# A four-layer attention network on one core: masks loaded as ready bfloat16 with the key weights asked for first, and two weight prefetches of the last block issued from SyncE

## The chip, the core and the metric

The kernel runs as one program on 1 core of one Trainium2 chip. The metric is the device time of one execution in microseconds, the median over runs. TensorE (PE) multiplies, VectorE (DVE) and ScalarE (ACT) do elementwise work, GpSimd (POOL) does elementwise work and issues DMAs through its own queue, and SyncE (SP) does nothing but issue DMAs. Each engine executes its instructions in order, so an instruction that waits holds up all that stand behind it on that engine.

## The reference

The input is a 2048 x 512 float32 sequence. Four layers follow each other, A, B, A, B, each added to its input after a layer norm:

```python
x = x + _A_ref(_layernorm(x), A_wq, A_wk, A_wv, A_wo)
x = x + _B_ref(_layernorm(x), B_wq, B_wk, B_wv, B_wo, B_beta)
x = x + _A_ref(_layernorm(x), A_wq, A_wk, A_wv, A_wo)
x = x + _B_ref(_layernorm(x), B_wq, B_wk, B_wv, B_wo, B_beta)
```

Layer A is full attention with 32 heads of 16 columns that share one key and one value head: `softmax(q k^T / 4) v`, all 2048 queries against all 2048 keys. Layer B cuts the sequence into 4 blocks of 512, does causal attention inside a block for each of 32 heads, and adds a linear attention over the blocks before it: a memory `M` of `phi(k)^T v` with its normaliser `z`, mixed in by a gate `sigmoid(beta)` for each head.

## The kernel before, in words

The sequence is worked in 4 blocks of 512 rows. Products that need float32 accuracy are made of three matmuls over rounded parts (high times high, high times low, low times high; `project`, L481), so each weight exists as a pair in a tile `w`: the rounded copy made by POOL (L204) and the rest, which DVE subtracts (L306, and L339 and L340 for the keys and values of layer A). `wload` loads a weight once through a staging tile `wst` (a pool of two buffers), splits it, and stores the pair in DRAM (`wd`, L310). Later uses load the pair back with one 512 KB DMA from POOL's queue (L293) into one of six `w` buffers. `wprefetch(n)` issues loads until n weights are ready, and `wget` hands them out in the order of one list.

The Python program emits instructions with a small clock model of its own (`clk`, `pe`, `on`), by which generators are interleaved (`par`, `weave`); a scheduler then sets each engine's order. Four stretches of time follow.

- The head. SP loads the first block of x, then constants (L217 to L239): an identity and selectors as `cs`, and masks and norm patterns as float32 in `wst` staging tiles, which DVE casts to bfloat16 tiles (L224 to L240). The key and value weights of layer A come after them in eight small-run DMAs (L336). Then `prep` runs: the layer norm of block 0 (`norm_stats` L516 to L530, `norm_tiles`: subtract and scale L538, transpose on PE L541, high part L544, low part L549), loads of x for the next block with its statistics, then `a_keys` (projection, split L577 and L579, the key tile `kst` L605 and L606, the values L611 and a bound on the norms L618) and `a_queries` of block 0 (four weights Aq0 to Aq3; split; the parts go to DRAM as `sd`, L656, with a guard row `mr`, L632 and L635). `a_load` fetches the head pairs of queries from `sd` as `qa` (L699, L700), and with them the first scores start (L101, L104), then the exponentials (ACT, L790).
- The body. For each block of queries ACT evaluates 128 exponentials of 128x1024 while PE multiplies; layer B of the block before is woven in beside.
- The last block of layer B (`side(NB - 1, 1, None, True)`), which has no layer A left beside it: `out_norm`, then `b_block` with `last=True`. There `begin()` projects q and k of the first head tile (`inputs(0)`), sends their parts to DRAM as `sb` (L931), loads the first head pair back as `qkb` (`b_load`, L971) and takes row maxima (L1001); `beside()` projects the values of the last two tiles and does `inputs(1)`. `par` picks among generators that are ready the one that keeps PE's tiling; one that is named `urgent` goes first. After both, `wprefetch(2)` asks for the weights Bq2 and Bk2.
- The eight head pairs of that block, the output projection (`out_norm` of `otb`), and the store.

The program uses eight completion semaphores in turn for the DMAs of SP, so each of them also waits for the landing of the eighth before it.

Of the kernel before, what the change touches and what calls it, by code (L numbers as in the profile page):

```python
# [29 lines left out]
F32 = mybir.dt.float32  # L30
# [24 lines left out]
C_ID, C_BM, C_SEL, C_MQ, C_MK, C_BN, C_BK, C_MV = 0, 128, 136, 144, 656, 784, 912, 1040  # L55
# [5 lines left out]
def shape_constants():  # L61
# [26 lines left out]
    return c  # L88
# [3 lines left out]
def net_kernel(ctx, tc, x_in, a_wq, a_wk, a_wv, a_wo, b_wq, b_wk, b_wv, b_wo, b_beta, cst, out):  # L92
# [76 lines left out]
    def st(shape, dt, tag):  # L169
        return one.tile(shape, dt, tag=tag, name=nm(tag))  # L170

    def tmp(n, shape, dt, tag):
        return pools[n].tile(shape, dt, tag=tag, name=nm(tag))

    def f(ap):
        return ap.bitcast(F32)
# [39 lines left out]
    cs = st([P, C_MQ], F32, "cs")  # L216
    nc.sync.dma_start(cs, cst[:, 0:C_MQ])  # L217
    c1 = tmp(2, [P, 512], F32, "wst")
    nc.sync.dma_start(c1, cst[:, C_MQ:C_MK])
    c2 = tmp(2, [P, 512], F32, "wst")[:, 0:C_MV - C_MK]  # L220
    nc.sync.dma_start(c2, cst[:, C_MK:C_MV])
    ident = cs[:, C_ID:C_ID + P]
    maskq = st([P, 512], BF16, "maskq")
    V.tensor_copy(maskq, c1)  # L224
    bmask = cs[:, C_BM:C_BM + 8]
    sel = [cs[:, C_SEL + i:C_SEL + i + 1] for i in range(7)]
    idb = st([P, P], BF16, "idb")
    V.tensor_copy(idb, ident)
    maskk = st([P, P], BF16, "maskk")
    V.tensor_copy(maskk, c2[:, C_MK - C_MK:C_MK - C_MK + P])  # L230
    bnq = st([P, 4, 32], BF16, "bnq")
    V.tensor_copy(bnq.rearrange("p t h -> p (t h)"), c2[:, C_BN - C_MK:C_BN - C_MK + P])
    bnk = st([P, P], BF16, "bnk")
    V.tensor_copy(bnk, c2[:, C_BK - C_MK:C_BK - C_MK + P])
    maskv = st([P, 4, P], BF16, "maskv")
    maskw = st([P, 4, P], BF16, "maskw")
    for m_, at in ((maskv, C_MV), (maskw, C_MW)):
        c3 = tmp(2, [P, 512], F32, "wst")
        nc.sync.dma_start(c3, cst[:, at:at + 512])  # L239
        V.tensor_copy(m_.rearrange("p c k -> p (c k)"), c3)  # L240
# [42 lines left out]
    def wload(kind, i, w=None, parts=""):  # L283
# [6 lines left out]
        if (kind, i) in parts_d:  # L290
            if w is None:
                w = tmp(6, [P, 2, 512], F32R, "w")
            G.dma_start(f(w), parts_d[kind, i])  # L293
            wq_["ready"].append((kind, i, w))
            return
# [21 lines left out]
    ahead_ = [2]  # L317

# [14 lines left out]
    w0 = tmp(2, [P, 512], F32, "wst")  # L333
    for r in range(8):
        src = (a_wv if r == 7 else a_wk).rearrange("(k p) c -> p k c", p=P)
        nc.sync.dma_start(w0.rearrange("p (k r c) -> p k r c", k=4, r=8)[:, :, r, :], src,  # L336
                          allow_slow_non_contiguous=True)
# [3 lines left out]
    nc.sync.dma_start(wkv_d, f(w1))  # L341
# [807 lines left out]
    def b_block(b, last, exact, norms):  # L1149
# [52 lines left out]
        yield from par(begin(), beside())  # L1202
        ahead_[0] = 2
        if last:
            wprefetch(2)
        if last:
            layout("b")
# [13 lines left out]
    def everything(exact):  # L1221
# [21 lines left out]
        def prep():  # L1243
            for b in range(NB):
                if exact:
                    xt, st_ = load_x(b), None
                elif b == 0:
                    xt, st_ = x_0, None
                else:
                    xt, st_ = ahead.pop(b)  # L1250
                for tiles in ((0, 1), (2, 3)) if st_ is None else ((0, 1, 2, 3),):
                    yield from norm_tiles(xt, tiles, clk["pe"] + LOAD, st_)
                if b < NB - 1 and not exact:
                    xt = load_x(b + 1)
                    ahead[b + 1] = xt, norm_stats(xt, (0, 1, 2, 3), clk["pe"] + LOAD)
                yield from a_keys(L, b, aw)
                if b == 0 or exact:
                    yield from a_queries(L, b, aw, not exact)
                evac_on[0] = "dve"
# [117 lines left out]
```

## Time and profile before

| | |
|---|---|
| median of 3 runs | 3129.34 us (3118.13 to 3132.39) |
| the profiled execution | 3124.81 us, span 3123.0 us |
| first matmul of the key projection (L481) | starts at 21.03 us |
| first scores of layer A (L101) | start at 46.28 us |
| first exponential (ACT L790) | starts at 47.22 us |
| last row of layer A's exponentials | starts at 2926.52 us |
| PE without work in the last block | 7.55 us, until 2979.24 us |
| mean granted PE clock | 0.976 |

Times in the timeline are from the span's start. A row gives start, duration, engine, line, operation and tiles, the number of instructions merged into it, and in brackets how long the engine was idle before it and what released it. Durations of pipelined instructions overlap: the step from one start to the next is the real cost of one in a run of equal ones.

### The profile page before, as it was taken

How to read it: one execution, taken by the hardware profiler on the slowest of the kernel's cores; microseconds unless marked ns; L12 is line 12 of the kernel's file. 1: busy time of each engine (PE TensorE's matmuls, PEld its weight loads, DVE VectorE, ACT ScalarE, POOL GpSimd, SP SyncE). 2: the span in 40 equal slices, each digit the busy share in tenths (PEclk: the TensorE clock that was granted, in tenths of full speed). 3: DMA queues.
4: the chain of work that ended last, by engine and by line, in shares of the span. 5: the costliest groups of instructions: out<-in, count | busy, mean ns of one | idle time of the engine just before them, and what ended most of it. 6: DMA issues, size and time to landing. Idle time of an engine off the chain costs nothing.

```text
span 3123.0 us, 115586 instructions
## 1 busy us (share of the span) xinstructions
PE 2776.1 (89%) x51746; PEld 1324.5 (42%) x51746; DVE 1581.4 (51%) x4515; ACT 2323.0 (74%) x2519; POOL 278.4 (9%) x437
## 2 busy tenths in 40 slices
PE   6899888999898998889998898988998899898977
PEld 3444443445443453344544344434443445343543
DVE  6644345534555435564455545456345643555465
ACT  4788777886788767787688878668688887888433
POOL 2001120001000010000100010000000001000111
PEclk9999999999999999999999999999999999999978
DMA  5212231113311233112422142311331113211331
GB/s 156 79 53 81 91 121 47 40 61 108 102 40 42 68 106 95 39 43 71 136 78 73 38 137 96 122 48 51 115 97 45 42 30 127 66 42 46 127 106 38
DMA packets 153596, 242.30 MB, mean 78 GB/s; under 512 B 26272, under 2 KB 101888, under 8 KB 153088
## 3 DMA queue, kind: packets, MB, share of 16 engines
q1 hardware_dynamic: 124672, 132.03, 14.2%
q0 software_dynamic: 28416, 102.77, 10.3%
q8 instruction: 407, 6.67, 0.9%
q14 instruction: 101, 0.83, 0.1%
HBM read 164.21 MB, written 70.52 MB: 75 GB/s over the span
## 4 chain that ended last, share of the span: by engine, by line
PE 38%; ACT 24%; issue 18%; DVE 10%; DMA 6%; POOL 2%; SPq 1%; DVEq 0%; ACTq 0%; POOLq 0%
ACT pa L790 20%; PE bank L101 18%; PE bank L481 13%; PE bank L104 7%; ACT pa L1066 3%; DVE mo L1030 3%; DMA sb<-parts 3%; DMA xt<-in_A_x_dram 1%; DVE parts L579 1%; DMA qkb<-sb 1%; POOL parts L577 1%; DMA wst<-in_B_wk_dram 0%; PE bank L541 0%; DVE qf L559 0%; DVE m L1001 0%
## 5 line engine op out<-in xcount | busy, mean ns | idle before, releaser
L790 ACT ACTIVATE pa<-bank 128x1024 f32<-128x1024 f32 x2048 | 1952.1, 1041 | 458.2 <-PE bank L104 451.9
L104 PE MATMUL bank<-pa,va 64*17 64x512 f32 x14336 | 1101.9, 598 | 0.0
L101 PE MATMUL bank<-pa,va 64*17 64x512 f32 x2048 | 1057.7, 597 | 8.6 <-DVE ts L828 8.0
L101 PE MATMUL bank<-qa,kst 49*32 49x512 f16 x2048 | 741.5, 381 | 159.2 <-ACT pa L790 108.2
L104 PE MATMUL bank<-qa,kst 49*32 49x512 f16 x14336 | 816.8, 386 | 1.9 <-DVE qmx L634 1.9
L1030 DVE CUSTOM_DVE_ANT_0 mo<-bank,maskq 128x256 bf16<-128x256 f32 (+3 forms) x896 | 438.6, 490 | 297.6 <-PE bank L104 239.8
L104 PEld LDWEIGHTS <-kst 49*32 49x32 f16 x14336 | 224.3, 90 | 502.5 <-issue 490.9
L101 PE MATMUL bank<-qkb 48*32 48x384 f16 (+6 forms) x1472 | 331.3, 305 | 94.7 <-DVE m L1030 33.7
L1066 ACT ACTIVATE pa<-bank 128x1024 f32<-128x1024 f32 x320 | 317.4, 1033 | 82.9 <-PE bank L104 79.7
L104 PE MATMUL bank<-qkb 48*32 48x512 f16 (+7 forms) x6720 | 354.1, 311 | 12.4 <-DVE m L1001 10.8
L101 PEld LDWEIGHTS <-kst 49*32 49x32 f16 x2048 | 172.3, 91 | 382.6 <-issue 354.3
L481 PE MATMUL bank<-xh,w 128*128 128x512 f32 x832 | 296.9, 416 | 9.7 <-DVE w L339 4.5
L104 PEld LDWEIGHTS bank<-pa,va 64*17 64x17 f32 x14336 | 256.7, 94 | 26.1 <-DVE t L829 12.1
L481 PE MATMUL bank<-w,xh 128*128 128x512 f32 x752 | 244.6, 407 | 3.7 <-issue 2.0
L101 PEld LDWEIGHTS bank<-pa,va 64*17 64x17 f32 x2048 | 187.7, 94 | 105.4 <-issue 16.7
L104 PEld LDWEIGHTS <-qkb 50*32 50x32 f16 (+1 forms) x6720 | 151.1, 93 | 186.2 <-issue 177.7
L293 POOL DMA_DIRECT2D w<-wd x154 | 85.4, 554 | 1390.8 <-PE bank L481 1207.9
L481 PEld LDWEIGHTS bank<-xh,w 128*128 128x128 f32 x832 | 158.9, 191 | 85.3 <-issue 41.8
L101 PEld LDWEIGHTS <-qkb 48*32 48x32 f16 (+1 forms) x1472 | 123.5, 93 | 130.2 <-issue 86.3
L559 DVE COPY qf<-bank 128x512 f32<-128x512 f32 x91 | 62.8, 690 | 213.9 <-PE bank L481 213.9
L104 PE MATMUL bank<-pa,vb 128*17 128x384 f32 (+3 forms) x1920 | 165.3, 447 | 4.0 <-ACT pa L1066 3.6
L481 PE MATMUL bank<-xl,w 128*128 128x512 f32 x416 | 167.6, 403 | 0.2 <-DVE xl L549 0.2
(171 smaller groups left out, 2679.3 us busy)
## 6 DMA issues: line engine op xcount, KB each, us to landing
w<-wd POOLq DMA_DIRECT2D x154, 512.0 KB, 5.0
sb<-parts SPq DMA_DIRECT2D x192, 128.0 KB
qkb<-sb SPq DMA_DIRECT2D x256, 96.0 KB
wd<-w POOLq DMA_DIRECT2D x24, 512.0 KB, 4.0
x<-xt SPq DMA_DIRECT2D x48, 256.0 KB
xt<-x SPq DMA_DIRECT2D x48, 256.0 KB
qa<-sd SPq DMA_DIRECT2D x176, 66.0 KB
xt<-in_A_x_dram SPq DMA_DIRECT2D x40, 256.0 KB
```

Source lines behind the costliest of these rows:

```text
L101: nc.tensor.matmul(*a, **k)
L104: tc.keep_in_program_order(nc.tensor.matmul(*a, **k))
L293: G.dma_start(f(w), parts_d[kind, i])
L481: T.matmul(ps, lhsT=l_(kt), rhs=r_(kt), start=n == 0, stop=n == 11)
L559: V.tensor_copy(x, ps)
L577: G.tensor_scalar(parts[:, 0, :], x, up, 0.0, op0=ALU.mult, op1=ALU.add)
L579: V.scalar_tensor_tensor(parts[:, 1, :], x, up, parts[:, 0, :], op0=ALU.mult, op1=ALU.subtract)
L790: A.activation(x, sc, AF.Exp, scale=scale)
L1030: V.tensor_tensor_reduce(out=mo[:, 0:nk], in0=ps[:, o_:o_ + nk], in1=maskq[:, 512 - nk:512], op0=ALU.add, op1=ALU.max, scale=1.0, scalar=- ...
L1066: A.activation(e, sc, AF.Exp, scale=0.25 if exact else 0.25 / (UPB * UPB))
```

## The change

Four things change in the code.

1. The constants. The host packs all masks and the bfloat16 identity as bfloat16 pairs into float32 words (`shape_constants`), so that `cst` has 576 bytes of float32 and 4096 bytes of bfloat16 for each of 128 partitions, where it had 8256 bytes of float32. Two loads bring them straight into two tiles, `halves`: a small one with the identity, `maskk`, `bnq` and `bnk`, and a large one with `maskq`, `maskv` and `maskw`. The seven casts on DVE are gone, and the names are now views of these tiles.
2. The key and value weights of layer A. They come right after the small constants, ahead of the large masks, in five DMAs instead of eight: for each of the four row tiles one DMA writes the 16 key columns seven times (a source with a step of 0), and one DMA brings the values. The staging tile `w0` is now the first user of its pool. The store of the split pair (`wkv_d`) moves from right behind the split into `prep`, behind the load of block 1.
3. `prep`. The statistics of the next block (`norm_stats`) are emitted after `a_keys` and `a_queries` of this block; the loads of its x stay where they were.
4. The last block. `begin()` is passed to `par` as `urgent`, and the prefetch of two weights after it (Bq2 and Bk2) is issued from SP instead of POOL.

```diff
+C_ID, C_BM, C_SEL, C_HALF = 0, 128, 136, 144
+C_IB, C_MK, C_BN, C_BK, C_MQ, C_MV = 144, 272, 400, 528, 656, 1168
...
-    cs = st([P, C_MQ], F32, "cs")
-    nc.sync.dma_start(cs, cst[:, 0:C_MQ])
-    c1 = tmp(2, [P, 512], F32, "wst")
-    nc.sync.dma_start(c1, cst[:, C_MQ:C_MK])
...
-    V.tensor_copy(maskq, c1)
...
-    for m_, at in ((maskv, C_MV), (maskw, C_MW)):
-        c3 = tmp(2, [P, 512], F32, "wst")
-        nc.sync.dma_start(c3, cst[:, at:at + 512])
-        V.tensor_copy(m_.rearrange("p c k -> p (c k)"), c3)
...
+    nc.sync.dma_start(halves[0][0], cst[:, halves[0][1]:halves[1][1]])
+    w0 = tmp(2, [P, 512], F32, "wst")
+    w0_ = w0.rearrange("p (k r c) -> p k r c", k=4, r=8)
+    for k in range(4):
+        src = bass.AP(tensor=a_wk.tensor, offset=a_wk.offset + k * P * DH, ap=[[DH, P], [0, 7], [1, DH]])
+        nc.sync.dma_start(w0_[:, k, 0:7, :], src, allow_slow_non_contiguous=True)
+    nc.sync.dma_start(w0_[:, :, 7, :], a_wv.rearrange("(k p) c -> p k c", p=P), allow_slow_non_contiguous=True)
+    nc.sync.dma_start(halves[1][0], cst[:, halves[1][1]:halves[1][1] + (C_N - C_MQ) // 2])
+    small, masks = (x.bitcast(BF16) for x, _ in halves)
...
-            G.dma_start(f(w), parts_d[kind, i])
+            (nc.sync if w_sync[0] else G).dma_start(f(w), parts_d[kind, i])
...
-        yield from par(begin(), beside())
+        first = begin()
+        yield from par(first, beside(), urgent=first if last else None)
         ahead_[0] = 2
         if last:
+            w_sync[0] = True
             wprefetch(2)
+            w_sync[0] = False
...
                     xt = load_x(b + 1)
-                    ahead[b + 1] = xt, norm_stats(xt, (0, 1, 2, 3), clk["pe"] + LOAD)
+                    t_ = clk["pe"] + LOAD
+                    if b == 0:
+                        nc.sync.dma_start(wkv_d, w1.bitcast(F32))
                 yield from a_keys(L, b, aw)
                 if b == 0 or exact:
                     yield from a_queries(L, b, aw, not exact)
+                if b < NB - 1 and not exact:
+                    ahead[b + 1] = xt, norm_stats(xt, (0, 1, 2, 3), t_)
```

The order of instructions shows what moves. In the head, SP's queue before, from the constants on (`wst_161` is the key and value weight, `gv` the gate, `xt_319` to `xt_325` block 1 of x):

```order
L217 DMA cs_89<-in_cst_dram 128x144
L219 DMA wst_91<-in_cst_dram 128x512
L221 DMA wst_93<-in_cst_dram 128x384
L349 DMA gv_174<-in_B_beta_dram 128x1x1 x4
L239 DMA wst_107<-in_cst_dram 128x512
L239 DMA wst_110<-in_cst_dram 128x512
L349 DMA gv_174<-in_B_beta_dram 128x1x1 x3
L336 DMA wst_161<-in_A_wk_dram 128x4x16 x7
L336 DMA wst_161<-in_A_wv_dram 128x4x16
L349 DMA gv_174<-in_B_beta_dram 128x1x1
L211 DMA xt_319<-in_A_x_dram 128x512
```

and the same stretch now, where `wst_94` is the key and value weight and lines have shifted by a few:

```order
L221 DMA cs_89<-in_cst_dram 128x144
L226 DMA halves_6_91<-in_cst_dram 128x256
L231 DMA wst_94<-in_A_wk_dram 128x7x16 x4
L232 DMA wst_94<-in_A_wv_dram 128x4x16
L233 DMA halves_7_92<-in_cst_dram 128x768
L346 DMA gv_152<-in_B_beta_dram 128x1x1 x8
L215 DMA xt_297<-in_A_x_dram 128x512
```

The weight now stands ahead of the large masks and the gates, and nothing that it waits for on DVE stands before it. On DVE in the head, the subtraction that finishes Aq0 (`w_205`) and Aq1 (`w_212`) before:

```order
L516 BN_STATS s_115_334<-xt_323 128x6
L359 RECIPROCAL over_186<-over_186 128x8
L306 TENSOR_TENSOR w_205<-wst_203,w_205 128x512
L517 BN_AGGR mv_327<-s_115_334 128x2
L516 BN_STATS s_116_337<-xt_325 128x6
L517 BN_AGGR mv_327<-s_116_337 128x2
L519 TENSOR_SCALAR ve_340<-mv_327 128x4
L521 TENSOR_SCALAR sh_342<-ve_340 128x4
L523 TENSOR_SCALAR yi_344<-sh_342 128x4
L306 TENSOR_TENSOR w_212<-wst_210,w_212 128x512
```

and now (`w_183` is Aq0, `w_190` Aq1, `xt_303` the last tile of block 1, `kmx_180` the bound on the keys):

```order
L513 BN_STATS s_156_676<-xt_303 128x6
L608 COPY va_15_111<-bank 128x4x16
L514 BN_AGGR mv_666<-s_156_676 128x2
L516 TENSOR_SCALAR ve_679<-mv_666 128x4
L615 TENSOR_REDUCE kmx_180<-bank 128x1
L308 TENSOR_TENSOR w_183<-wst_181,w_183 128x512
L308 TENSOR_TENSOR w_190<-wst_188,w_190 128x512
L576 SCALAR_TENSOR_TENSOR parts_323<-qf_318,parts_323 128x512
```

Both subtractions now stand together, behind all four statistics of block 1 and behind the two readings of the key projection; Aq0's stood in front of the fourth before. In the last block, POOL's queue before, from the second tile's key weight on (`w_52294` is Bk1, `w_52686` and `w_52688` are Bq2 and Bk2, `w_53021` and `w_53084` Bq3 and Bk3):

```order
L293 DMA w_52294<-wd_5945 128x1024
L293 DMA w_52686<-wd_6239 128x1024
L577 TENSOR_SCALAR parts_52283<-qf_52281 128x512
L293 DMA w_52688<-wd_6622 128x1024
L577 TENSOR_SCALAR parts_52310<-qf_52308 128x512
L293 DMA w_53021<-wd_7564 128x1024
L293 DMA w_53084<-wd_8046 128x1024
```

and SP's queue now at the same place (`w_52665` and `w_52667` are Bq2 and Bk2, `sb_52265` the parts of q and `sb_52292` those of k of the first head tile):

```order
L858 DMA xt_55077<-x_173 128x512
L295 DMA w_52665<-wd_6218 128x1024
L928 DMA sb_52265<-parts_52262 8x16x512 x3
L295 DMA w_52667<-wd_6601 128x1024
L928 DMA sb_52292<-parts_52289 8x16x512 x3
L968 DMA qkb_19_119<-sb_52265 48x2x512 x2
```

The two loads have left POOL and stand on SP in front of the stores that the first row maxima wait for. On PE the rows of the last block are the same as before, word for word up to the numbers of the names, so `urgent` moves nothing there.

More of the change, by code (lines that the diff above doesn't have):

```diff
@@ L53 @@
 TA1 = 110e3
-C_ID, C_BM, C_SEL, C_MQ, C_MK, C_BN, C_BK, C_MV = 0, 128, 136, 144, 656, 784, 912, 1040
+C_ID, C_BM, C_SEL, C_HALF = 0, 128, 136, 144
+C_IB, C_MK, C_BN, C_BK, C_MQ, C_MV = 144, 272, 400, 528, 656, 1168
 S_X, S_H, S_L, S_G = 0, 4, 5, 6
@@ L87, in shape_constants @@
         c[64 * i + 48, C_SEL + S_G] = -GUARD_K
-    return c
+    c[:, C_IB:C_IB + P] = np.eye(P)
+    u = np.ascontiguousarray(c[:, C_HALF:]).view(np.uint32)
+    u = ((u + 0x7fff + ((u >> 16) & 1)) >> 16).astype(np.uint16)
+    return np.concatenate([c[:, 0:C_HALF], u.view(np.float32)], axis=1)
 @with_exitstack
@@ L215, in net_kernel @@
     x_0 = load_x(0)
-    cs = st([P, C_MQ], F32, "cs")
-    nc.sync.dma_start(cs, cst[:, 0:C_MQ])
-    c1 = tmp(2, [P, 512], F32, "wst")
-    nc.sync.dma_start(c1, cst[:, C_MQ:C_MK])
-    c2 = tmp(2, [P, 512], F32, "wst")[:, 0:C_MV - C_MK]
-    nc.sync.dma_start(c2, cst[:, C_MK:C_MV])
+    cs = st([P, C_HALF], F32, "cs")
+    nc.sync.dma_start(cs, cst[:, 0:C_HALF])
+    halves = []
+    for a, z in ((C_IB, C_MQ), (C_MQ, C_N)):
+        h_ = st([P, (z - a) // 2], F32, f"halves{a}")
+        halves.append((h_, C_HALF + (a - C_HALF) // 2))
@@ L222, in net_kernel @@
+    small, masks = (x.bitcast(BF16) for x, _ in halves)
     ident = cs[:, C_ID:C_ID + P]
-    maskq = st([P, 512], BF16, "maskq")
-    V.tensor_copy(maskq, c1)
     bmask = cs[:, C_BM:C_BM + 8]
     sel = [cs[:, C_SEL + i:C_SEL + i + 1] for i in range(7)]
[L227 to L236, printed above, removed]
-    for m_, at in ((maskv, C_MV), (maskw, C_MW)):
-        c3 = tmp(2, [P, 512], F32, "wst")
-        nc.sync.dma_start(c3, cst[:, at:at + 512])
-        V.tensor_copy(m_.rearrange("p c k -> p (c k)"), c3)
+    idb, maskk = small[:, 0:P], small[:, P:2 * P]
+    bnq, bnk = small[:, 2 * P:3 * P].rearrange("p (t h) -> p t h", t=4), small[:, 3 * P:4 * P]
@@ L241, in net_kernel @@
+    maskq = masks[:, 0:512]
+    maskv = masks[:, 512:1024].rearrange("p (c k) -> p c k", c=4)
+    maskw = masks[:, 1024:1536].rearrange("p (c k) -> p c k", c=4)
     ones = st([P, 32], BF16, "ones")
@@ L317, in net_kernel @@
     ahead_ = [2]
+    w_sync = [False]
     def wget(kind, n, ahead=None):
@@ L332, in net_kernel @@
     wkv_d = dram.tile([P, 2, 512], F32, tag="wkv_d", name="wkv_d")
[L333 to L337, printed above, removed]
     w1 = tmp(6, [P, 2, 512], F32R, "w")
@@ L340, in net_kernel @@
     V.tensor_tensor(w1[:, 1, :], w0, f(w1[:, 0, :]), op=ALU.subtract)
-    nc.sync.dma_start(wkv_d, f(w1))
     wq_["ready"].append(("Akv", 0, w1))
```

## The prediction

> **What bounds the kernel now.** I read the page first (span, busy shares), then the stretches in time, then the timeline and the chain of waits at the two ends.
>
> ```profile
> span 3123.0 us, 115586 instructions
> PE 2776.1 (89%) x51746; PEld 1324.5 (42%) x51746; DVE 1581.4 (51%) x4515; ACT 2323.0 (74%) x2519; POOL 278.4 (9%) x437
> L790 ACT ACTIVATE pa<-bank 128x1024 f32<-128x1024 f32 x2048 | 1952.1, 1041 | 458.2 <-PE bank L104 451.9
> ```
>
> PE is busy for 89% of the span, and the 2048 exponentials wait almost only for PE. This body is left as it was: past the first 100 us and up to the last block the order of all engines is the old one. What can change is when the body starts, and how long the last block takes after it. At the start, the stretches and the timeline:
>
> ```profile
> 10.00:20.00 10.00, 3.94 (x16) 3.06 (x16) 7.57 (x30) 2.35 (x4) 1.55 (x2) 1.00 0.58 105
> ```
>
> ```profile
> 14.07 3.71 SPq L336 DMA_DIRECT2D wst<-in_A_wk_dram  x7
> 15.21 2.67 DVE L549 TENSOR_TENSOR xl<-bank,xh 128x512 fp32r<-128x512 f32 x4
> 16.57 0.59 ACT L544 CAST xh<-bank 128x512 fp32r<-128x512 f32 x1 [0.27 <-PE bank L541]
> 20.45 0.43 DVE L339 CAST w<-wst 128x512 fp32r<-128x512 f32 x1 [2.58 <-DMA wst<-in_A_wv_dram]
> 21.03 0.77 PE L481 MATMUL bank<-xh,w 128*128 128x512 f32 x1 [4.50 <-DVE w L339]
> 46.28 0.61 PE L101 MATMUL bank<-qa,kst 49*32 49x512 f16 x1 [2.29 <-DMA qa<-sd]
> ```
>
> (Columns of the stretches: length, then busy time of PE, its weight load, DVE, ACT and POOL, granted PE clock, DMA share, GB/s.) Between 10 and 20 us PE works for 3.94. The normalised block is complete when ACT ends at 16.57 + 0.59 = 17.16, but the first projection waits until 21.03 for a weight whose first load was issued at 14.07. The scores start at 46.28. At the other end:
>
> ```profile
> 2961.02 0.53 POOL L293 DMA_DIRECT2D w<-wd  x1 [14.96 <-PE bank L481]
> 2962.36 4.82 SPq L931 DMA_DIRECT2D sb<-parts  x6
> 2963.59 0.58 POOL L293 DMA_DIRECT2D w<-wd  x1 [1.25 <-PE bank L481]
> 2965.68 1.23 POOL L293 DMA_DIRECT2D w<-wd  x2 [0.85 <-PE bank L481]
> 2966.17 10.23 DMA sb<-parts
> 2979.24 0.58 PE L101 MATMUL bank<-qkb 48*32 48x512 f16 x1 [7.55 <-DMA qkb<-sb]
> ```
>
> The fifth row is of the chain of waits: the last store of the first head tile's parts, issued at 2966.17, takes 10.23 us to land, the load behind it comes later still, and PE has nothing to do for 7.55 us.
>
> **Part by part, the head.** The change removes seven casts and moves the weight loads forward. (The third row is of the chain of waits.)
>
> ```profile
> 0.74 1.82 SPq L211 DMA_DIRECT2D xt<-in_A_x_dram  x4
> 11.66 1.00 DVE L538 TENSOR_SCALAR xn<-xt,mv,yn 128x512 f32<-128x512 f32 x2
> 17.83 2.51 DMA wst<-in_A_wv_dram
> 20.92 0.69 DVE L340 TENSOR_TENSOR w<-wst,w 128x512 fp32r<-128x512 f32 x1
> 26.24 0.59 ACT L557 COPY qf<-bank 128x512 f32<-128x512 f32 x1 [2.81 <-PE bank L481]
> ```
>
> SP has issued x at 2.56; two constants, then five weight DMAs at the old 3.71 / 7 = 0.53 each, or half as much again for their wider shape, end at 6.1 to 7.5, and with the 2.51 us that the last of them took to land the weight is there at about 10. DVE asks for it only behind the first two scalings, 11.66 + 1.00, so 2.7 us of slack cover a slower load. On DVE seven casts go, three of them as wide as the one of 0.43 at 20.45, and that one and the 0.69 behind it come in before the last scaling; I call that even. So the first projection can start at about 17.2, when ACT's last high part is there, and not at 21.03: 3.8 us earlier. It took from 21.03 to 26.24, 5.2 us; its result then reaches ACT at 22.4.
>
> The next link is the four query weights.
>
> ```profile
> 26.27 0.64 DVE L306 TENSOR_TENSOR w<-wst,w 128x512 fp32r<-128x512 f32 x1
> 28.90 0.69 DVE L516 BATCH_NORM_STATS2 s<-xt 128x6 f32<-128x512 f32 x1 [1.90 <-DMA xt<-in_A_x_dram]
> 30.61 1.15 DVE L306 TENSOR_TENSOR w<-wst,w 128x512 fp32r<-128x512 f32 x1
> 31.19 0.63 ACT L651 ACTIVATE sqq<-qf 128x512 bf16<-128x512 f32 x1
> 31.96 0.68 DVE L618 TENSOR_REDUCE kmx<-bank 128x1 f32<-128x512 f32 x1
> 33.30 0.84 DVE L605 TENSOR_SCALAR xn<-parts,cs 128x512 f32<-128x512 f16 x1
> 34.18 0.75 DVE L606 SCALAR_TENSOR_TENSOR kst<-parts,cs,xn 128x512 f16<-128x512 f16 x1
> 35.94 0.67 DVE L632 TENSOR_SCALAR mr<-bank 8x512 f16<-8x512 f32 x1
> 36.61 0.67 DVE L579 SCALAR_TENSOR_TENSOR parts<-qf,parts 128x512 f16<-128x512 f32 x1
> 37.31 3.52 DMA sd<-parts
> ```
>
> ```profile
> 12.96 0.17 DVE yn L530
> 3039.86 4.91 PE bank L481 x21
> ```
>
> Before, the second subtraction (30.61) stood behind statistics that waited for x until 28.90. Now both stand behind the key bound: ACT copies the keys to 23.0 and squares them (0.63), PE multiplies (0.4, an estimate), DVE reduces (0.68): 24.8; two subtractions of 0.64 end at 26.1, where the second ended at 31.76. From there DVE's own queue is the path: parts 0.67, 0.84 and 0.75 for the key tile, ten dependent small steps like the one at 12.96, 0.2 with the way to the next (2.0), then guard row, its maximum and one scaling (0.67, 0.67, 0.54), then the query parts (0.67): 32.9. PE needs the two query projections meanwhile, 12 matmuls at 4.91 / 21 = 0.234, 2.8 us each, and is done in time. The store behind those parts was issued at 37.31; now it can be at 33.0. Landing, the load back and the first scores follow as before, so they start 4.3 us earlier, near 42. **Head: -4.3 us.** As PE and ACT are then fed in the old way, I take it as kept to the end.
>
> What is moved past what: SP's load of x for the later queries now stands in front of the second store of parts and of the first `qa` loads, and waits for a scaling on DVE that comes right before those parts; it adds its issue alone, about 0.4 us. The gates come later and their exponential stands in ACT's queue before the key copy; by the issue times above the loads end by about 14 (an estimate), and ACT asks at 17.2. The bounds: at best the key path gives the 5.6 us by which the second weight is earlier; at worst x of block 1 is late (the fourth rival, +1.6). Views in place of tiles, the packed constants and the later `wkv_d` store cost nothing: the casts' readers read the same bfloat16, and the store's reader comes hundreds of microseconds later.
>
> **Part by part, the last block.** `urgent` changes no row on PE, so it is priced at nothing. The two loads of 512 KB leave POOL for SP.
>
> ```profile
> DMA packets 1950, 4.09 MB, mean 273 GB/s; under 512 B 177, under 2 KB 1214, under 8 KB 1949
> q0 software_dynamic: 822, 3.01, 62.5%
> q1 hardware_dynamic: 1127, 1.06, 24.9%
> ```
>
> These are the queues from 2962 to 2977: POOL's moved 3.01 MB, SP's 1.06, of which the six stores of 128 KB are 0.79. Before, the stores shared the engines with POOL's loads all along, at 1.06 MB in 15 us = 71 GB/s. Now SP's queue holds load, three stores, load, three stores (1.83 MB), and POOL's next load comes only behind its issue at 2965.68, 1.23 us long, so that its data start about 2967. Up to there SP's queue is alone: 4.5 us from 2962.4 at 273 GB/s are 1.2 MB, that is the first load, three stores, and some of the second load. The 0.6 MB left are 0.2 of load and 0.39 of stores. The stores in company take 0.39 / 71 = 5.5 us, the rest 0.7: landed at about 2973.2, where it was 2976.4. **Last block: -3 us.** Bounds: nothing gained, since the bytes are the same, or -5 if the engines share more evenly; +3.8 if both loads merely stand in front of the stores, 2 x 0.52 MB at 273 GB/s. The loads also wait on SP for a free buffer, until 2961.02 and 2963.59, with the stores queued behind; those parts leave POOL and DVE only at 2962.3 and later, so the waits cost at most the 0.4 us of an issue.
>
> The shorter stall could also spare PE its slow clock.
>
> ```profile
> 44.00:46.00 2.00, 0.00 (x0) 0.00 (x0) 0.27 (x1) 0.59 (x1) 0.59 (x1) 1.00 0.61 190
> 46.00:48.00 2.00, 1.72 (x19) 0.73 (x20) 0.84 (x2) 0.78 (x1) 0.87 (x2) 0.55 0.94 315
> 2974.00:2976.00 2.00, 0.00 (x0) 0.00 (x0) 0.00 (x0) 0.00 (x0) 0.00 (x0) 0.71 1.00 306
> 2980.00:3000.00 20.00, 16.69 (x437) 8.20 (x423) 17.79 (x39) 3.95 (x5) 0.00 (x0) 0.50 0.24 70
> ```
>
> In the head, 2.3 us without matmuls were enough for a clock of 0.55 behind them, so the 4.5 us that I leave in the last block keep it halved, as from 2974 on: no gain. The Trainium skill, "TensorE: Matmul & The Clock Gate", Part 1, says that the clock halves after an idle window of about 3.4 us that runs free; by that a stall of 4.5 us would hold a whole window one time in three, and the sum would be the larger one of the third rival. The row at 46.00 speaks against it.
>
> **The sum.** -4.3 - 3.0 = -7.3 us. The profiled execution took 3124.81 for a span of 3123.0; the 1.8 us around it stay. So 3117.5 on that scale; the median of the runs lies 4.5 above it, and 3129.3 - 7.3 gives **3122.0**. A measurement of this kernel can tell about 0.5%, 15.6 us, from no change.
>
> **The rivals.**
>
> 1. The queue does not matter (chance 0.20). For it: the same bytes go through the same 16 engines, which were 1.00 busy at 2974. Against: POOL's queue was empty before 2965.68. The stall stays 7.55, the head gives its 4.3: 3125. It is what the Trainium skill says in "DMA: Bandwidth & Descriptors", section "Issuing engines are not separate DMA queues": several issuing engines interleave on the same DMA engines, and only issue time is saved. The fifteen microseconds at 273 GB/s agree that they interleave; how a queue's own order tells, no row here shows.
> 2. The loads stand in the way (0.08). On SP they go out ahead of the stores, which wait their 3.8 us: 3129. For it: the stores are in the same queue. Against: the first load has over a microsecond's start.
> 3. The stall shrinks below what lowers the clock (0.14). From 2980 to 3000, at clock 0.50, DVE was busy 17.79, so at most 2.2 us were PE's alone, and about 1 more behind 3000. With the best ends, -5.6 - 5 - 3.2 = -13.8: 3115.5.
> 4. Slower (0.08): the statistics of block 1 now stand in front of both subtractions. If the last tile of x lands where it did, at 28.9 and not near 20 (issued by 17, and 2.5 to 3.5 us on the way as in the rows above), DVE reaches the subtractions at 31 and ends the second at 32.3; the 6.8 us of queue behind it bring the store to 39 and the scores to 47.9, +1.6, and with a last block unchanged 3131. It decides from a landing at about 23 on; then DVE waits for x instead of the key projection. For it: SP holds eight small gate loads in front of x, each waiting for the eighth DMA before it. Against: by my times those loads are over by about 14, and the x buffers are free before 17.2.
>
> **How the numbers follow.** The forecast has 0.50. The range holds rivals 1, 2, 4 and the forecast with the scatter of the three runs shown, and part of rival 3: 3110 to 3132. Faster by over 0.5% (below 3113.7) needs rival 3 and a little more: 0.16. Slower by over 0.5% (above 3145) is in no case's reach but by an unseen loss: 0.04. Within 0.5%: 0.80.
>
> **What would show it.** Right: the first key matmul near 17.2 and waiting for ACT, the first scores near 42, the wait of PE for `qkb` near 4.5 us, and stores that land by 2973 on the old scale. Wrong: a weight cast that waits for its load, statistics of x that wait past 23, scores later than 44, a stall in the last block of 7 us or more, or a clock that stays at 1.00 there.

## The result, and the profile after

| | before | after |
|---|---|---|
| median, 8 runs each | 3122.82 us (3117.43 to 3132.39) | 3137.49 us (3126.82 to 3141.35) |
| ratio after / before | | 1.0034, 95% interval 1.0019 to 1.0049 |
| span of the profiled execution | 3123.0 us | 3130.8 us |
| first key projection starts | 21.03 us | 17.53 us |
| first scores / first exponential | 46.28 / 47.22 us | 47.86 / 49.76 us |
| ACT without exponentials before the 81st | 7.07 us | 18.48 us |
| 101st exponential starts | 172.69 us | 182.40 us |
| last exponential of layer A starts | 2926.52 us | 2935.28 us |
| PE waits for the first pair of the last block | 7.55 us | 6.68 us |

The change is slower by 0.34%, some 10.6 us of 3123. It is inside the half per cent that was called no change, but not on the forecast side, and the median lies outside the range. The 8 runs of before have a median 6.5 us below that of the 3 runs that the forecast started from.

The page of the changed kernel shows the same work as before. PE, which bounds the kernel, is busy for 1.5 us more, so most of the 7.8 us between the spans is not work:

```profile
PE 2777.6 (89%) x51746; PEld 1329.1 (42%) x51746; DVE 1579.7 (50%) x4508; ACT 2321.8 (74%) x2519; POOL 278.7 (9%) x435
```

So it is waiting, and its place is found by counting exponentials: the k-th of the 2048 (256 for each of four blocks of queries in each of the two layers A, not 128) is the same work in both kernels, and the difference of its starts is the delay up to there. It is +2.5 us at the first, -1.2 at the 80th, +10.3 at the 81st, +9.7 at the 101st, +5.4 at the 512th and +8.8 at the last. **The one large step is a jump of 11.4 us between the 80th and the 81st.** Behind it the difference drifts by a few microseconds both ways. Such drift need be no effect of the change: run e8 below has the program of the kernel before up to the last block, and its profile is 5.1 us behind at the last exponential. The first 64 exponentials need the keys of block 0 alone, the next 8 those of block 1, the next 8 those of block 2, and the 81st is the first that needs the keys of block 3.

The timeline of the kernel before at this place (ACT's exponentials, the projection of block 3's keys, its copy on DVE, the 81st exponential):

```profile
133.74 7.50 ACT L790 ACTIVATE pa<-bank 128x1024 f32<-128x1024 f32 x8
140.60 0.50 PE L481 MATMUL bank<-xh,w 128*128 128x512 f32 x1
143.77 0.69 DVE L559 COPY qf<-bank 128x512 f32<-128x512 f32 x1 [4.50 <-PE bank L481]
148.31 1.94 ACT L790 ACTIVATE pa<-bank 128x1024 f32<-128x1024 f32 x2 [3.19 <-PE bank L104]
```

and of the changed kernel:

```profile
133.59 6.54 ACT L787 ACTIVATE pa<-bank 128x1024 f32<-128x1024 f32 x7
141.20 1.09 PE L538 MATMUL bank<-cs,xn 128*128 128x128 f32 x8
142.38 0.69 DVE L513 BATCH_NORM_STATS2 s<-xt 128x6 f32<-128x512 f32 x1 [2.00 <-DMA xt<-in_A_x_dram]
147.60 0.80 PE L478 MATMUL bank<-xh,w 128*128 128x512 f32 x1 [0.78 <-DVE xh L544]
153.50 0.69 DVE L556 COPY qf<-bank 128x512 f32<-128x512 f32 x1 [2.31 <-PE bank L478]
158.61 1.94 ACT L787 ACTIVATE pa<-bank 128x1024 f32<-128x1024 f32 x2 [3.76 <-PE bank L108]
```

Before, the projection starts 0.64 us ahead of the end of the 80th exponential (133.74 + 7.50 = 141.24), takes 3.17 us to the copy, and 4.54 pass from there to the 81st: 7.07. Now the end is at 140.13; 1.07 us later PE transposes three of the four tiles of block 3, which takes 6.40 us with their high and low parts on DVE (a row of later statistics stands in front of these parts, waits for its x until 142.38 and holds them by under a microsecond); the projection takes 5.90 to the copy, at a clock that the windows below show lowered; 5.11 more to the 81st: 18.48. Of the 11.41 us between the two stretches, 8.11 are the later start of the projection (0.64 before the end of the 80th, now 7.47 behind it), 2.73 its longer run and 0.57 the rest. The tiles that used to be normalised beside running exponentials are normalised while ACT has nothing to do. The windows there (the third figure from the end is the granted clock):

```profile
140.00:150.00 10.00, 5.16 (x33) 3.12 (x34) 6.67 (x14) 0.14 (x1) 0.00 (x0) 0.85 0.27 79
150.00:160.00 10.00, 7.74 (x38) 4.26 (x38) 5.32 (x19) 2.02 (x3) 2.85 (x4) 0.67 0.29 103
```

PE's order of instructions says why. Row numbers in the program, transposes of block 3 and the start of its key projection, before and now:

```
1250 L541 MATMUL bank_158<-cs_5_89,xn_297_1643 128x128 x4
1302 L541 MATMUL bank_158<-cs_5_89,xn_302_1707 128x128 x4
1392 L541 MATMUL bank_158<-cs_5_89,xn_310_1764 128x128 x4
1463 L541 MATMUL bank_158<-cs_5_89,xn_316_1846 128x128 x4
1518 L481 MATMUL bank_158<-xh_41_156,w_44_170 128x512
...
1491 L538 MATMUL bank_146<-cs_5_89,xn_300_1745 128x128 x4
1514 L538 MATMUL bank_146<-cs_5_89,xn_311_1893 128x128 x4
1515 L538 MATMUL bank_146<-cs_5_89,xn_313_1927 128x128 x4
1516 L538 MATMUL bank_146<-cs_5_89,xn_314_1935 128x128 x4
1517 L478 MATMUL bank_146<-xh_33_144,w_35_149 128x512
```

They stood spread over 200 rows of scores; now three of them stand in a row right before the projection.

In the head, the timeline of the changed kernel (the gate, the copy of the keys, the first statistics of block 1, then the four query weights: subtractions of Aq0 and Aq1, loads of Aq2 and Aq3, POOL's high part of the second query projection, rounding and subtractions of Aq2 and Aq3; the first scores):

```profile
17.53 0.79 PE L478 MATMUL bank<-xh,w 128*128 128x512 f32 x1 [0.67 <-ACT xh L541]
23.70 0.21 ACT L348 ACTIVATE gv<-gv 128x8 f32<-128x8 f32 x1 [6.22 <-DMA gv<-in_B_beta_dram]
23.81 0.57 ACT L554 COPY qf<-bank 128x512 f32<-128x512 f32 x1
24.54 0.65 DVE L513 BATCH_NORM_STATS2 s<-xt 128x6 f32<-128x512 f32 x1
28.57 1.28 DVE L308 TENSOR_TENSOR w<-wst,w 128x512 fp32r<-128x512 f32 x2
30.69 1.54 POOL L301 DMA_DIRECT2D wst<-in_A_wq_dram  x2
37.71 1.01 POOL L574 TENSOR_SCALAR parts<-qf 128x512 f16<-128x512 f32 x1 [2.44 <-ACT qf L554]
38.80 1.71 POOL L208 TENSOR_SCALAR w<-wst 128x512 fp32r<-128x512 f32 x2
39.96 1.69 DVE L308 TENSOR_TENSOR w<-wst,w 128x512 fp32r<-128x512 f32 x2 [0.51 <-POOL w L208]
47.86 0.60 PE L105 MATMUL bank<-qa,kst 49*32 49x512 f16 x2
49.76 3.77 ACT L787 ACTIVATE pa<-bank 128x1024 f32<-128x1024 f32 x4 [3.22 <-PE bank L108]
```

The last gate load in the chain of waits of the changed kernel (start, duration):

```profile
13.99 9.48 DMA gv<-in_B_beta_dram
```

The last two query weights of the kernel before, loads and subtractions:

```profile
29.72 0.81 POOL L299 DMA_DIRECT2D wst<-in_A_wq_dram  x1
33.82 0.80 POOL L299 DMA_DIRECT2D wst<-in_A_wq_dram  x1
34.85 1.09 DVE L306 TENSOR_TENSOR w<-wst,w 128x512 fp32r<-128x512 f32 x1
38.78 0.67 DVE L306 TENSOR_TENSOR w<-wst,w 128x512 fp32r<-128x512 f32 x1
```

The first projection starts 3.5 us earlier, and the scores start 1.6 us later. The gates land at about 23.5 and hold ACT's copy of keys that PE had ready at about 22.2. The statistics of block 1 stand in front of both subtractions, which end at 29.85. Only then are both staging tiles `wst` free, so both of the last weights are asked for together, at 30.69. Their rounding on POOL then stands behind the high part of the second query projection, which comes only at 37.71, and follows it at 38.80 without waiting for a load. The subtractions start at 39.96, where they came one by one, at 34.85 and 38.78. The first scores follow PE's projections with these weights without a wait, at 47.86; before, PE had finished them at 43.99 and waited 2.29 for `qa`.

At the other end, the timeline of the changed kernel, with the two prefetches on SP's queue, POOL's loads, and PE's first matmul on the first pair:

```profile
2971.41 0.32 SPq L295 DMA_DIRECT2D w<-wd  x1
2975.18 0.33 SPq L295 DMA_DIRECT2D w<-wd  x1
2976.30 1.23 POOL L295 DMA_DIRECT2D w<-wd  x2 [1.01 <-PE bank L478]
2988.98 0.58 PE L105 MATMUL bank<-qkb 48*32 48x512 f16 x1 [6.68 <-DMA qkb<-sb]
```

The last store of parts in its chain of waits (start, duration):

```profile
2976.91 9.38 DMA sb<-parts
```

The stretch behind it (busy time of PE, PEld, DVE, ACT and POOL, then the granted clock, the DMA share and GB/s):

```profile
2990.00:3010.00 20.00, 16.36 (x430) 8.30 (x418) 17.20 (x38) 4.51 (x5) 0.00 (x0) 0.57 0.23 66
```

And the DMA packets between 2972.5 and 2977 (count, MB, rate; those of SP's queue):

```profile
DMA packets 529, 0.96 MB, mean 214 GB/s; under 512 B 34, under 2 KB 385, under 8 KB 528
q1 hardware_dynamic: 528, 0.95, 68.4%
```

The last store takes 9.38 us in place of 10.23, PE waits 6.68 in place of 7.55, and the clock behind it is still about half.

### The profile page after: what moved, and what is told of

Read it like the earlier page. It is cut to its first block, busy times and chain, and to the rows that moved or that the text cites. A ratio compares the mean times of both kernels' runs of the same rounds, so it can differ in the third digit from the quotient of the medians.

```text
span 3130.8 us, 115571 instructions
## 1 busy us (share of the span) xinstructions
PE 2777.6 (89%) x51746; PEld 1329.1 (42%) x51746; DVE 1579.7 (50%) x4508; ACT 2321.8 (74%) x2519; POOL 278.7 (9%) x435
## 4 chain that ended last, share of the span: by engine, by line
PE 37%; ACT 23%; issue 22%; DVE 10%; DMA 5%; POOL 2%; SPq 1%; DVEq 0%; ACTq 0%; POOLq 0%
ACT pa L787 19%; PE bank L105 17%; PE bank L478 13%; PE bank L108 7%; DVE mo L1027 3%; ACT pa L1063 3%; DMA sb<-parts 2%; DMA qkb<-sb 1%; POOL parts L574 1%; DVE parts L576 1%; PE bank L538 1%; DVE qf L556 0%; DVE m L998 0%; SPq L928 0%; DVE t L1092 0%
## 5 line engine op out<-in xcount | busy, mean ns | idle before, releaser
L1027 DVE CUSTOM_DVE_ANT_0 mo<-bank,halves 128x256 bf16<-128x256 f32 (+3 forms) x896 | 438.5, 489 | 296.1 <-PE bank L108 238.9
```

Source lines behind the costliest of these rows:

```text
L1027: V.tensor_tensor_reduce(out=mo[:, 0:nk], in0=ps[:, o_:o_ + nk], in1=maskq[:, 512 - nk:512], op0=ALU.add, op1=ALU.max, scale=1.0, scalar=- ...
```

## The experiments

Three theories stood at first: the moved statistics set another interleaving (order theory), the later gates and loads of x delay everything (head theory), or the loss is only in where stretches of a lowered clock fall (clock theory). "The stretch" is the time of ACT between the end of the 80th and the start of the 81st exponential. Ratios are to the kernel before, run beside each on the same chip (e1 to e4, e5 to e8 and e9 to e12 on one chip each); the other columns are read from the profiled execution of each run.

| run | ratio, 95% interval | first exponential | the stretch | 101st exponential | PE waits, last block |
|---|---|---|---|---|---|
| before | | 47.22 | 7.07 | 172.69 | 7.55 |
| after | 1.0034 (1.0019 to 1.0049) | 49.76 | 18.48 | 182.40 | 6.68 |
| e1 after, statistics back | 1.0014 (0.9999 to 1.0030) | 48.85 | 7.09 | 177.73 | 6.97 |
| e2 before, statistics moved | 1.0027 (1.0014 to 1.0041) | 49.11 | 18.71 | 183.32 | 7.33 |
| e3 after, last block back | 1.0042 (1.0026 to 1.0059) | 46.76 | 17.77 | 178.61 | 7.55 |
| e4 before, constants and weights alone | 1.0016 (1.0001 to 1.0032) | 47.68 | 7.08 | 176.48 | 8.07 |
| e5 e1 with the gates later | 0.9999 (0.9987 to 1.0010) | 45.61 | 7.14 | 169.58 | 6.94 |
| e6 before, emitted late only | 1.0010 (0.9998 to 1.0023) | 46.72 | 7.07 | 172.24 | 7.82 |
| e7 before, model told late only | 1.0055 (1.0035 to 1.0075) | 49.08 | 19.20 | 184.96 | 7.87 |
| e8 before, last block alone | 1.0009 (0.9996 to 1.0021) | 47.64 | 7.08 | 174.41 | 6.93 |
| e9 after, TA0 = 40e3 | 1.0016 (1.0003 to 1.0030) | 50.87 | none | 178.08 | 6.99 |
| e10 before, TA0 = 50e3 | 0.9991 (0.9980 to 1.0003) | 47.49 | none | 173.18 | 8.36 |
| e11 e5 with TA0 = 50e3 | 0.9989 (0.9975 to 1.0003) | 47.02 | none | 169.78 | 7.19 |
| e12 e1, gates from ACT's queue | 1.0013 (0.9999 to 1.0027) | 51.38 | 7.13 | 177.54 | 7.01 |

### One part at a time

The statistics back at their old place in the changed kernel (e1):

```diff
-                    t_ = clk["pe"] + LOAD
+                    ahead[b + 1] = xt, norm_stats(xt, (0, 1, 2, 3), clk["pe"] + LOAD)
...
-                if b < NB - 1 and not exact:
-                    ahead[b + 1] = xt, norm_stats(xt, (0, 1, 2, 3), t_)
```

> The changed kernel with the statistics of the next block emitted at their old place; the loads and the last block stay changed. Order theory (the moved statistics alone give the new interleaving of the first 160 us, and the keys of block 3 then come too late for the 81st exponential): the idle stretch of ACT before that exponential falls from 18.5 us to about 7, as it was before the change, and the time falls by 8 to 12 us to 3122 to 3130, ratio to before 0.997 to 1.002. Head theory (the later gates and x loads delay everything and the stretch follows from that): the stretch stays at 15 us or more and the ratio at about 1.003. Clock theory (the loss is in where the slow clock windows fall in the body): the stretch changes little, the ratio anywhere from 1.000 to 1.005.

The stretch is 7.09 us, as the order theory had it. The ratio falls to 1.0014, less than the 8 to 12 us that were expected: some of the loss seems to stay, though the interval reaches 0.9999.

The same lines the other way round, in the kernel before and alone (e2):

> The kernel before with only the statistics of the next block emitted later. Order theory: the idle stretch before the 81st exponential grows from 7 us to 16 to 20, the time by 8 to 13 us, ratio 1.0025 to 1.004. Head theory: the first key projection still starts at 21 us, nothing else is late, ratio 0.999 to 1.001. Clock theory: the same as the head theory.

```profile
129.66 11.32 ACT L790 ACTIVATE pa<-bank 128x1024 f32<-128x1024 f32 x12
159.69 1.94 ACT L790 ACTIVATE pa<-bank 128x1024 f32<-128x1024 f32 x2 [3.92 <-PE bank L104]
```

The 80th exponential ends at 140.98 and the 81st starts at 159.69: 18.71, and 1.0027. The old constants, the old weight loads and the old last block are all in this kernel, so the moved statistics alone make the stretch, and the head theory falls for it. The clock theory falls too: it gave this kernel an unchanged time, and the stretch comes and goes with the edit. The lowered clock that lies on the projection in the stretch is worth 2.73 of the 11.41 us above.

The last block back (e3); the loads alone (e4) take these lines and those of e1 out of the changed kernel together:

```diff
-        first = begin()
-        yield from par(first, beside(), urgent=first if last else None)
+        yield from par(begin(), beside())
...
-            w_sync[0] = True
             wprefetch(2)
-            w_sync[0] = False
```

> The changed kernel with the last block as before (prefetch on POOL, no urgent generator). Order theory: the stretch before the 81st exponential is 18.5 us as in the changed kernel, ratio 1.003 to 1.0045, since the last block gave 1 to 3 us that now go. If the last block brought nothing, the ratio is that of the changed kernel, 1.0034. The wait of PE for the first head pair of the last block is 7.5 us again if SP's queue had shortened it (to 6.7 in the changed kernel).

> The kernel before with the packed constants and the weights first alone: statistics and last block as before. Order theory: the stretch before the 81st exponential is about 7 us; what is left is the head alone. If the head gains as predicted (first scores near 42 us), ratio 0.9985; if the gates, that now land behind the weights, hold the key copy and the statistics, first scores at 45 to 48 us and ratio 1.000 to 1.001. Head theory: the loads are the loss, ratio 1.003.

The parts add up, each within some 0.15%: loads +0.16% (e4), statistics +0.27% (e2), 0.43 together, beside 0.42 for the run that has both without the last block (e3) and 0.34 with it. The loads lose something as well: the head theory is right for a part, of 0.01 to 0.32%.

DVE's rows in e4, the last statistics of block 1 and the subtractions of Aq0 and Aq1:

```profile
26.18 0.66 DVE L513 BATCH_NORM_STATS2 s<-xt 128x6 f32<-128x512 f32 x1
27.77 1.28 DVE L308 TENSOR_TENSOR w<-wst,w 128x512 fp32r<-128x512 f32 x2
```

Here the statistics are emitted at their old place, and all four still stand in front of both subtractions. In e2, where they are emitted later, the subtraction of Aq0 (26.78) stays in front of the fourth (27.95). So that order on DVE in the head comes with the loads, not with the third edit.

### The statistics: their place on DVE, or the time that the program's model gives them

The move does two things. The program emits the statistics later, and the model's clock, by which `weave` chooses between scores and preparation, has them ready later. e6 emits them late and tells the model the old time; e7 emits them early and tells it the late time:

```diff
-                    ahead[b + 1] = xt, norm_stats(xt, (0, 1, 2, 3), clk["pe"] + LOAD)
+                    t_ = on("dve", clk["pe"] + LOAD, 4 * 700 + 2300)
...
+                    c_ = clk["dve"]
+                    ahead[b + 1] = xt, norm_stats(xt, (0, 1, 2, 3), 0.0)[0:2] + (t_,)
+                    clk["dve"] = c_
```

```diff
+                    ahead[b + 1] = xt, norm_stats(xt, (0, 1, 2, 3), 0.0)
...
+                    st_ = ahead[b + 1][1]
+                    ahead[b + 1] = xt, (st_[0], st_[1], on("dve", t_, 4 * 700 + 2300))
```

> The kernel before with the statistics emitted late, but the program's clock model told that they were done at the old time. PE's rows are then those of the kernel before. Planner theory (the time that the model puts on the statistics, not their place on DVE, makes the keys of block 3 late): the idle stretch before the 81st exponential is 7 us, ratio 0.999 to 1.001. DVE theory (the statistics come late on DVE and hold the next block): stretch 12 us or more, ratio 1.002 or more.

> The kernel before with the statistics emitted at their old place, but the clock model told that they are done later, as in the changed kernel. PE's rows from the first scores on are then those of the changed kernel. Planner theory: stretch 17 to 19 us, ratio 1.002 to 1.004. DVE theory: stretch 7 us, ratio 1.000.

ACT's exponentials around the 81st, e6:

```profile
133.02 9.33 ACT L790 ACTIVATE pa<-bank 128x1024 f32<-128x1024 f32 x10 [0.16 <-PE bank L104]
149.42 1.94 ACT L790 ACTIVATE pa<-bank 128x1024 f32<-128x1024 f32 x2 [3.19 <-PE bank L104]
```

and e7:

```profile
129.56 11.31 ACT L790 ACTIVATE pa<-bank 128x1024 f32<-128x1024 f32 x12
160.07 1.94 ACT L790 ACTIVATE pa<-bank 128x1024 f32<-128x1024 f32 x2 [4.13 <-PE bank L104]
```

7.07 and 19.20 us, 1.0010 and 1.0055, with intervals that do not touch. The number in the model makes the stretch, not the place where the lines are emitted. A place on DVE alone was not tried: from 50 us up to the 81st exponential DVE's rows in e6 follow the order of the kernel before, and those of e7 the order of e2, so the number moves PE's order and DVE's together. (e7 lost more than e2; their intervals overlap, so no more is read from that.)

### The head

The gates emitted behind the preparation, so that x of block 1 follows the masks on SP (e5, from e1):

```diff
+    gates = {}
+    def gate_tiles():
...
+        gates.update(gv=gv, g1=g1, over=over)
...
+        gate_tiles()
         layout("pa")
```

> The changed kernel with the statistics at their old place, and with the gates (their eight small loads, the exponential on ACT and the eight small steps on DVE) emitted behind the head, so that block 1 of x follows the large masks on SP. Head theory, now as a chain: gates and x come in at 23 to 24 us, the key copy on ACT and the statistics on DVE wait for them, both subtractions stand behind, the two staging buffers come free only then, and the last two query weights are loaded at 30 us and split at 40, later than before. Then this kernel copies the keys at about 22, subtracts by 24, loads the last two query weights by 26, splits them by 36, has its first scores at 43 to 45 and its 17th exponential at 64 us or earlier, and comes out at 0.997 to 1.000 of the time before (the same kernel with the gates in place: 1.0014, 17th exponential at 70). Clock theory (what is lost in the first 70 us is only the place of a slow clock window, at 58 us with the loads changed): first scores earlier by at most 1 us, ratio 1.001 to 1.002.

The last two query weights (load, subtraction), the first scores and the first exponential of e5:

```profile
27.95 1.53 POOL L301 DMA_DIRECT2D wst<-in_A_wq_dram  x2
35.99 1.29 DVE L308 TENSOR_TENSOR w<-wst,w 128x512 fp32r<-128x512 f32 x2
44.98 0.39 PE L105 MATMUL bank<-qa,kst 49*32 49x512 f16 x1
45.61 1.03 ACT L790 ACTIVATE pa<-bank 128x1024 f32<-128x1024 f32 x1
```

These links come earlier than in the changed kernel, if less than expected (loads at 27.95, not by 26; the key copy at 23.49, not at 22), the 17th exponential starts at 62.16 (e1: 70.24, before: 64.93), and the ratio is 0.9999 against 1.0014. This supports the chain from gates and x to the query weights. It moves both at once; which of the two holds how much was not separated. The clock differs as well: from 20 to 30 us and from 55 to 70 us e5 had 1.00 and e1 0.77, and of the 8.1 us at the 17th exponential 3.2 are there at the first (45.61, in e1 48.85).

The gates at the very start from ACT's queue (e12, from e1):

```diff
-            nc.sync.dma_start(gv[:, 4 * p + t:4 * p + t + 1], src, allow_slow_non_contiguous=True)
+            nc.scalar.dma_start(gv[:, 4 * p + t:4 * p + t + 1], src, allow_slow_non_contiguous=True)
```

> The changed kernel with the statistics at their old place and the eight gate loads issued from ACT's queue at the very start, where ACT has nothing to do, in place of SP's. Head theory (x of block 1 behind the gates on SP, and ACT and DVE behind their landing, are what holds the key copy and both subtractions): key copy at 22 to 23 us, subtractions by 23, first scores 43 to 45, 17th exponential at 60 to 63, ratio 0.997 to 1.000. If the gates land late from this queue too, the high parts of block 0 on ACT and the split of the key weight on DVE wait for them: first projection after 18, ratio 1.001 or more.

ACT's first work and the first key projection of e12:

```profile
15.48 1.28 ACT L348 ACT_TABLE_LOAD   x1 [15.48 <-DMA halves<-in_cst_dram]
26.45 0.80 PE L478 MATMUL bank<-xh,w 128*128 128x512 f32 x1 [0.68 <-ACT xh L541]
```

The second branch came true, and by more than it said: the projection starts 8.9 us later than in the changed kernel.

### The last block

Its two edits alone (e8), the lines taken out in e3 put into the kernel before:

> The kernel before with the last block's change alone (prefetch on SP, begin as urgent). If the queue gives what the factorial of the first four runs says (0.08%), ratio 0.9985 to 1.0000, the wait of PE for the first head pair 6.5 to 6.9 us in place of 7.55, stores of the first head tile landed under 1 us earlier. If the queue gives nothing: 1.0000, 7.5 us. If the forecast's 3 us were right: the wait 4.5 us, ratio 0.999.

PE waits 6.93 us, and the ratio cannot be told from 1. Over all runs the wait is 7.33 to 8.36 us with the prefetch on POOL (7 profiles, mean 7.79) and 6.68 to 7.19 with it on SP (7 profiles, mean 6.96). The queue gives 0.8 us of wait, and no time that these runs can measure.

### Preparing the blocks earlier

One number of the planner lowered, in the changed kernel (e9, shown), and to 50e3 in the one before (e10) and in e5 (e11):

```diff
-TA0 = 60e3
+TA0 = 40e3
```

> The changed kernel, whole, with one number of the planner lowered (TA0, from 60e3 to 40e3), so that the preparation of blocks 1 to 3 is interleaved earlier: PE's rows now have the projection of the keys of block 3 after 71 exponentials, where it stood after the 80th. Planner theory (the 81st exponential waits for keys that stand too late in PE's order, and nothing else of the changed kernel costs as much): the stretch before the 81st exponential goes from 18.5 us to under 2, the 101st exponential comes 14 to 18 us earlier than in the changed kernel, ratio 0.997 to 1.000. DVE theory (late statistics hold the keys wherever PE's rows stand): the wait turns up elsewhere before the 81st exponential, ratio 1.002 to 1.004.

> The kernel before with the same number lowered to 50e3, by which the keys of block 3 stand after 71 exponentials too. Planner theory: the stretch of 7 us before the 81st exponential goes as well, ratio 0.997 to 0.999. If those 7 us are a wait that only moves (the keys' work takes PE's time wherever it stands), the ratio is 0.999 to 1.001.

> The run with the gates emitted behind the head (packed constants, weights first, last block as changed, statistics at the old place) with that number at 50e3. If both causes are found, head and keys add up: 3 us from the head and 6 to 7 from the stretch, ratio 0.996 to 0.998. If the stretch comes back as waits elsewhere: 0.999 to 1.001.

In all three the stretch is gone. Of the changed kernel's loss about half is made good (1.0016, over the 1.000 that the planner theory gave, and with an interval that overlaps the changed kernel's): another wait stands before the 52nd exponential of e9, where PE, at a lowered clock, projects the keys of an earlier block. That exponential in the timeline, and the stretch before it:

```profile
118.29 1.02 ACT L787 ACTIVATE pa<-bank 128x1024 f32<-128x1024 f32 x1 [8.70 <-PE bank L108]
```

```profile
110.00:120.00 10.00, 8.12 (x52) 4.78 (x52) 5.43 (x14) 1.71 (x3) 0.62 (x1) 0.66 0.08 28
```

In e10 the 7 us of the kernel before go too, and the 101st exponential starts at 173.18, where it started at 172.69: the wait only moved. So the stretch is not a pure loss that an earlier order returns whole. I read this as the cost of preparation that runs without exponentials beside it, wherever it stands; no run isolates that. e11, the best version, has 0.9989 with an interval up to 1.0003, where 0.996 to 0.998 was expected if both causes had been found: no version that clearly beats the kernel before was found.

## Why the prediction was wrong, point by point

- **"Past the first 100 us and up to the last block the order of all engines is the old one."** This step failed, and with it "I take it as kept to the end". PE's order differs up to row 1517, which runs at 147.6 us, and there it is the order that costs: 11.4 us before the 81st exponential. The prediction looked at the moved statistics on DVE in the head only. That the model's clock sees the move as well, and `weave` spreads the work of blocks 1 to 3 by it, was not in the forecast nor in any rival: the sum puts the body at nothing. e2, e6 and e7 show it.
- **The first projection at 17.2.** Right: 17.53, and it waits for ACT's high part as foretold.
- **Its result on ACT at 22.4; gate loads over by about 14, x "landed near 20".** PE had the result at about 22.2, as forecast, but ACT waited for the gates until 23.70 and DVE began the statistics at 24.54. The last gate load was issued at 13.99, close to the forecast; the term that was left out is its 9.48 us of landing. When x landed in the changed kernel no row shows, since DVE was held by the gates.
- **The second subtraction at 26.1.** 29.85: the fourth rival, but with the gates as what comes late. It gave scores at 47.9 and +1.6 us; measured 47.86. That this fits so well is partly luck: it let the second subtraction end at 32.3 and the scores wait for stored query parts, while PE reached the scores straight from the projections with the last two weights. Its chance of 0.08 rested on an estimate of eight small loads by their issue times.
- **"PE needs the two query projections, and is done in time."** Wrong in two ways. There are four of them in front of the first scores, and the last two weights wait for the two staging tiles and then, on POOL, behind the second projection. And the projections ran in part at a lowered clock (below), not at the 0.234 us for one matmul. The gain of 4.3 us became a loss of 2.5 at the first exponential of this profile.
- **Last block, -3 us.** The mechanism held, the size did not: 0.85 us of landing and 0.87 of wait. The mis-sized term is "alone at 273 GB/s": SP's queue alone moved 0.95 MB in 4.5 us, 214 GB/s, so more was left to share with POOL's loads: 9.38 us to the landing where the sum had 7.0. The 0.25 MB by which this falls short of the forecast's 1.2 account for most of it: from 2977 to 2986.4 SP's queue moved 1.17 MB beside POOL's 1.88, that is 124 GB/s, at which they take 2.0 us (an estimate from these figures). The first rival (the queue does not matter) is nearer. The Trainium skill, "DMA: Bandwidth & Descriptors", "Issuing engines are not separate DMA queues", says that transfers from several issuing engines interleave on the same DMA engines and only issue time is saved; the mean waits of 7.79 and 6.96 us agree but for those 0.8 us.
- **`urgent` nothing, clock still halved in the last block.** Right: 0.57 from 2990 to 3010.
- **The bottom line.** Slower, and the main cause is in no rival; the fourth has a part of what went wrong in the head. The starting median was 6.5 us too high as well, which made the range too high, not too low.

What stays open: the medians differ by 14.7 us and the ratio by 10.6, the profiled executions by 7.8 (the changed kernel's took 3132.64, 4.9 under its median). The runs also give their mean granted clock, and the time goes with it: among the 93 runs of the kernel before beside the experiments, with a mean of 0.9775, each 0.001 less goes with 2.5 us more. The eight runs of the changed kernel have 0.9753, so, as an estimate from these figures, some 5 of its 10.6 us go with a lower clock. Whether the longer stretch brings that clock about is not shown; in the two profiles the first 250 us have 0.97 before and 0.95 after, the body up to 2900 us 0.99 in both. And how much of e4's 0.16% is the gates, the x loads or the staging tiles is not settled.

## What to carry to other kernels

Where a program plans its own order with a clock model, moving a piece of emitted code can change the plan more than the engine's queue: compare the orders to the row where they meet again, find the time of that row in the trace, and price every stretch up to there. Count the k-th instruction of a long row of equal ones in both traces: a jump in the difference of its starts finds the place of a loss in one look, and a second run with the same jump tells it from drift. Work that is prepared beside the running exponentials is hidden until its last tiles slip behind them; here the last three tiles of one block did, and the wait grew from 7.07 to 18.48 us.

## What the runs showed of the hardware

The lowered clock in the head differs between executions of the same code. The windows from 20 to 40 us of the changed kernel, of the run e3, whose head is the same program, and of the kernel before:

```profile
20.00:30.00 10.00, 6.51 (x22) 3.94 (x22) 5.92 (x21) 1.31 (x3) 1.68 (x3) 0.70 0.49 156
30.00:40.00 10.00, 7.40 (x23) 4.93 (x21) 6.36 (x20) 2.43 (x4) 5.05 (x8) 0.78 0.60 197
```

```profile
20.00:30.00 10.00, 6.79 (x25) 4.16 (x25) 6.51 (x22) 1.31 (x3) 2.26 (x4) 0.83 0.36 138
30.00:40.00 10.00, 7.08 (x24) 4.27 (x23) 8.66 (x22) 2.43 (x4) 6.43 (x9) 0.88 0.71 230
```

```profile
20.00:30.00 10.00, 8.67 (x31) 6.36 (x32) 5.57 (x19) 1.43 (x3) 2.22 (x4) 1.00 0.75 237
30.00:40.00 10.00, 7.66 (x30) 4.51 (x28) 9.89 (x26) 3.15 (x6) 6.54 (x11) 1.00 0.53 178
```

With 0.70 and 0.78 the first exponential starts at 49.76, with 0.83 and 0.88 at 46.76: three microseconds between two executions of one program, of which 0.6 are there already when PE goes on after the key copy (24.43 and 23.85). In the changed kernel the lowered clock follows an idle time of PE of 2.3 us. The old start at 21 us is no safeguard: before it PE is idle for 4.50 us in the kernel before, which then ran at 1.00, and in e6, whose PE rows are the same, the window is

```profile
20.00:30.00 10.00, 8.78 (x30) 6.43 (x31) 5.85 (x21) 1.43 (x3) 2.30 (x4) 0.67 0.75 237
```

Eight loads of 0.5 KB each, moved to the head of ACT's queue, delayed the first key projection from 17.54 us in e1 to 26.45 in e12, though they hold 4 KB in all: in this program they are not free for being small, and what stands behind them waits. How much of it is the loads themselves, how much the completion semaphores that they share with SP's loads, and how much the order on ACT and DVE behind them was not separated.
